# Window attention into two FF layers: group 4's softmax, five weight conversions and the second batch's v means written at other places

## The chip, the cores and the metric

The kernel runs on one core of one Trainium2 chip. The metric is device time in microseconds (us), the median of the runs. A profiled execution records what each engine does: TensorE (PE; its weight loads stand apart as PEld), VectorE (DVE), ScalarE (ACT), GpSimd (POOL) and SyncE (SP), which issues most DMAs.

## The reference, cut to what matters

```python
def _attn_ref(q, k, v):                       # (2, 8, 768, 64) each
    ...
    k_sum = k.reshape(B, H, nb, block, D).max(axis=3)      # block 32
    v_sum = v.reshape(B, H, nb, block, D).mean(axis=3)
    scores_l = scale * np.matmul(q, k.transpose(0, 1, 3, 2))
    mask_l = np.abs(pos[:, None] - pos[None, :]) < window  # 16
    scores_s = scale * np.einsum('bhsd,bhnd->bhsn', q, k_sum)
    scores_s = scores_s + np.log(block)
    scores_l_m = np.where(mask_l, scores_l, -1000000000.0)
    scores_all = np.concatenate([scores_l_m, scores_s], axis=-1)
    ...
    a = np.exp(scores_all)
    a = a / (np.sum(a, axis=-1, keepdims=True) + 1e-09)
    return np.matmul(a, np.concatenate([v, v_sum], axis=2))

def _moe_ref(x, w_in, w_out):                 # 1536 x 512, FF 2048
    h = np.maximum(x @ w_in, 0.0)
    return h * h @ w_out

def _moe2_ref(x, w_gate, w_val, w_out, rms_g):  # FF 1536
    ...
    return silu * val @ w_out
```

The result of the attention goes through `_moe_ref` and that through `_moe2_ref`.

## The kernel before

**Tiling.** The attention's 2 x 768 tokens are 12 groups of 128 tokens with all 8 heads; groups 0 to 5 are batch 0, groups 6 to 11 batch 1 (`GPB` is 6). A group has these steps: `scores` (32 matmuls into two PSUM tiles `s`), `softmax` (on VectorE two mask additions, a maximum `mx`; on ScalarE eight exponentials with sums, or for groups 5 and 9 a subtraction on VectorE and one exponential; then on VectorE the sum `sm` plus 1e-9, a reciprocal and the product `norm`), `ptrans` (8 transposes into two tiles `pps`, two ScalarE copies into `pT`), and `av` (32 matmuls into `xps`, then `xhi` by ScalarE and `xlo` by VectorE). `vload` loads a group's v rows into `vx`, which has four slots; groups alternate between slots 0, 1 and 2, 3, so a group's v rows cannot be loaded before the `av` of two groups earlier has read its slots. `qload` loads q for two groups, `qprep` transposes it (`qps`).

**FF layers.** Each fp32 operand is split into a high and a low part and each product is three matmuls (high by high, high by low, low by high). The first FF layer starts while the attention runs: its first round, four of 16 tiles of the inner size, goes over pairs of groups, `k_` from 0 to 5. For a pair `h_pair(k_, 0)` and `h_pair(k_, 2)` compute two inner tiles each (24 matmuls of 256 columns into `h0_k_f`; ScalarE takes the relu and VectorE the square, `r`; ScalarE `hhi` and VectorE `hlo` split it), and `y_pair(k_, 0)` and `y_pair(k_, 2)` multiply by the output weights (12 matmuls of 512 columns each). The attention of groups 4 to 11 is written between these calls. Behind the last pair, the rest of the first layer and the second run without attention.

**Weights.** A weight unit (`wi`, `wo`, later `wg`, `wv`, `wp`) is loaded raw as 64-bit words on SP's queue (512 KB), turned into fp32 by ScalarE (`conv_a`: `x`, `u`) and VectorE (`conv_b`, the "clamps": two tensor-scalars, L210 and L211, a scalar-tensor-tensor, L214, an integer addition, L217) and then split (`split`: a ScalarE cast, L223, and a VectorE subtraction, L224). Units 0 to 3 are `wi0` to `wi3`, units 4 to 7 `wo0` to `wo3`, and behind them come `wi4`, `wi5`, `wi6`, `wo4`, `wi7` and so on.

**What sets the order.** Every engine runs its instructions in one row. The row is made when the program is built: a scheduler takes the instructions as written and places each by an estimate of when it could start, so an instruction can move past others of its engine. `after(marks)` pins an instruction behind marked ones. The dictionary `FIRST` holds such pins for the units: the key (1, n) is `conv_a` of unit n, (2, n) is `conv_b`. PSUM tiles of the attention rotate through two tags with two buffers each, so the fifth tile reuses the buffer of the first.

The v means of batch 1 (`vs_mean`, `vmput`) are one matmul over `vsum`, which DMAs sum up, a VectorE copy and a GpSimd copy into `vx`.

Names such as `h0_3_0` read as pair 3, first tile; `xps1_8` is group 8's `av`. I call the time up to the start of group 5's transposes (71.57 us) stage 1, the time to the start of `h0_2_0` (82.87) stage 2, to the second part of `h0_3_0` behind group 10's q transposes (113.60) stage 3, and to the `xlo` matmul of `h0_4_0` (129.92) stage 4.

Of the kernel before, what the change touches and what calls it, by code (L numbers as in the profile page):

```python
# [15 lines left out]
ALU = mybir.AluOpType  # L16
# [16 lines left out]
def tile_window_attention_moe_moe2(  # L33
# [13 lines left out]
    nc = tc.nc  # L47
# [17 lines left out]
    GPB = S // P  # L65
# [154 lines left out]
    def split(x, nm):  # L220
# [4 lines left out]
        return hi, lo  # L225

    FIRST = {
        (2, 0): [("mx", 0)], (2, 2): [("mx", 2)], (2, 3): [("xlo", 1, 1)],
        (1, 1): [("qT", 2), ("pT", 1)], (1, 2): [("xhi", 0, 1)], (1, 3): [("exp", 2)],
    }  # L230

# [97 lines left out]
    mark = {}  # L329

    def after(*marks):
        es = ExitStack()
        for m in marks:
            es.enter_context(tc.issue_after(mark[m].ins))
        return es
# [74 lines left out]

    def vs_mean(b):
        ps = psA(f"vmean{b}", [K1, DM])[G0:K1]
        with after(("tr", GPB)):
            nc.tensor.matmul(ps, indv, vsum.rearrange("p h d -> p (h d)"), start=True, stop=True)
        vm = ap_.tile([K1, DM], F32, tag="vm", name=f"vm{b}", bufs=1)[G0:K1]
        state["vm"] = vm
        nc.vector.tensor_copy(vm, ps)
# [4 lines left out]
    def qload(g):  # L422
        b, r = divmod(g, GPB)
        state[("q", g)] = token_chunk(q, b, r // 2, f"qr{g}")
# [36 lines left out]
    def vmput(i0, n):  # L461
        nc.gpsimd.tensor_copy(vrows(i0, n), state["vm"].unsqueeze(1).to_broadcast([NB, n, DM]))
# [16 lines left out]
    def scores(g):  # L479
        b, r = divmod(g, GPB)  # L480
        qT = state[("qT", g)][:, :, (r % 2) * P : (r % 2 + 1) * P]
        sl = [psA(f"s{e}_{g}", [P, NPAIR, NK]) for e in range(2)]
        wide = [P, NPAIR, NK]
        if g < NPE:
            for s_ in sl:
                mh = mhi["mid" if r else "first"]
                nc.tensor.matmul(s_, identr, mh.unsqueeze(1).to_broadcast(wide), start=True, stop=False)
        for p in range(NPAIR):
            for x in range(2):
                for e in range(2):  # L490
                    u = (e + x) % 2
                    o = STEP * (2 * r + u)
                    rr = slice(QT * e, QT * e + QT)
                    with after(*((("av", 1),) if g == 3 else ())):
                        mark[("s", g)] = nc.tensor.matmul(  # L495
                            sl[e][QT * u : QT * u + QT, p, :],
                            qT[rr, p, QT * u : QT * u + QT],
                            kT[rr, p, o : o + NK],
                            start=g >= NPE, stop=g >= NPE,
                        )  # L500
        if g < NPE:
            for s_ in sl:
                mark[("s", g)] = nc.tensor.matmul(
                    s_, identr, mlo.unsqueeze(1).to_broadcast(wide), start=False, stop=True
                )
        state[("s", g)] = sl
# [44 lines left out]
    def ptrans(g):  # L551
        t = state.pop(("t", g))
        pT = ap_.tile([NK, H, P], F32, tag="pT", name=f"pT{g}", bufs=2)
        for hf in range(2):
            ps = psA(f"pps{g}_{hf}")
            for j in range(4):
                mark[("tr", g)] = nc.tensor.transpose(  # L557
                    ps[0:NK, j * P : (j + 1) * P], t[:, 4 * hf + j, :], ident
                )
            mark[("pT", g)] = nc.scalar.copy(pT[:, 4 * hf : 4 * hf + 4, :], ps[0:NK].rearrange("n (h s) -> n h s", h=4))  # L560
        state[("pT", g)] = pT
# [158 lines left out]
    def group(g):  # L720

        scores(g)
        if g > 3:
            vload(g)
        softmax(g)
        if g + 2 < NG and g % 2 == 0:
            qload(g + 2)
# [71 lines left out]
    def square(ps, nm):  # L799
        t = t2(f"r{nm}")  # L800
        nc.scalar.activation(t, ps, AF.Relu)  # L801
        nc.vector.tensor_tensor(t, ps, t, op=ALU.mult)  # L802
        return t


# [4 lines left out]
    def h_pair(k_, f):  # L810
        ps = psB.tile([P, CH], F32, tag="h", name=f"h0_{k_}_{f}", bufs=2)
        m = 2 * k_ % MT
        for j in range(2):
            units1.until(("wi", f + j))
            product(ps[:, G2 * j : G2 * (j + 1)], W[("wi", f + j)], xs[(1, 2 * k_ // MT)], m, m + 2)
        t = square(ps, f"0_{k_}_{f}")
        hq[(k_, f)] = hsplit(t, CH, f"0_{k_}_{f}")
# [22 lines left out]
    for k_ in range(NK2):  # L840
        g, last = 2 * k_ + 3, 2 * k_ + 3 >= NG
        h_pair(k_, 0)
        if k_ == 0:
            av(2)
            group(4)
        if not last:
            ptrans(g)
        h_pair(k_, 2)
        if not last:
            av(g)  # L850
        if g == GPB - 1:
            group(GPB)
        if g + 2 < NG:
            group(g + 2)
            if k_ == 0:
                for c in range(NC2):
                    prep_load(1, c)
                vs_load(1)
        y_pair(k_, 0)
        if g + 1 < NG:  # L860
            ptrans(g + 1)
        if g + 1 == GPB:
            vs_mean(1)
            vmput(0, 4)
        if k_ == 0:
            prep_begin(1)
            prep_k(1, 0)
            y_pair(k_, 2, (lambda: prep_k(1, 1), lambda: prep_k(1, 2)))
            prep_kend(1, nc.vector, 0, NW1)
        else:  # L870
            if g + 3 < NG:
                qprep(g + 3)
            y_pair(k_, 2)
        if g + 1 < NG:
            av(g + 1)
        if k_ == 0:
            qprep(GPB)
        elif g + 3 < NG:
            group(g + 3)
        if k_ == 2:  # L880
            units1.cap = NW - 3
            units1.load(units1.cap)
            units1.lim = len(units1.units)
            units1.behind = (("exp", 9), ("norm", 9))
        if k_ == NK2 - 1:
            units1.behind = ()
        for _ in range(TICKS[k_]):
            units1.tick()
        if not last and g == NG - 1:
            actx.close()  # L890
            rot["tags"] = ("a",)
            side["cb"] = ctx.enter_context(
                tc.tile_pool(name="cbpool", bufs=1, side="right", reuse_waits="tile")
            )
            grow = side["cb"].tile([P, DM], F32, tag="grow", name="grow")
            side["pool"] = hand.enter_context(
                tc.tile_pool(name="w2pool", bufs=1, side="right", reuse_waits="tile")
            )
            side["psum"] = ctx.enter_context(
                tc.tile_pool(name="psY2", bufs=1, space=PSUM, reuse_waits="tile")  # L900
            )
            nc.sync.dma_start(grow, rms_g.partition_broadcast(P))
            units1.cap = NW + NRIGHT - 3
# [256 lines left out]
```

## Time and profile before

| | us |
|---|---|
| median of 3 runs | 639.9 (639.51 to 640.55) |
| profiled execution | 640.56 |
| its span | 638.9 |
| PE busy | 623.5 (98%) |
| DVE busy | 458.3 (72%) |
| ACT busy | 365.0 (57%) |

The profiled execution is 1.66 longer than its span and 0.66 longer than the median. A matmul's row gives its own duration, which overlaps the next one's; the cost of a matmul in a sequence is the distance between starts. "Idle before" is the time that the engine stood, with the instruction that it waited for. PEclk is the granted clock of TensorE as a share of 2.4 GHz.

### The profile page before, as it was taken

What the parts mean: (1) busy time and instruction counts of PE and PEld (TensorE: products, weight loads), DVE (VectorE), ACT (ScalarE), POOL (GpSimd) and SP (SyncE); (2) the same over time, 40 slices, a digit from 0 to 9 for tenths busy, and PEclk for the clock granted to TensorE, in tenths of its full rate; (3) what the DMA queues carried; (4) which work ended last, traced back from release to release, by engine and by line L of the source; (5) the groups of instructions that cost most, each with busy time, mean ns of one, the idle gap of its engine ahead of it and who ended that gap; (6) DMA issues with size and microseconds to landing.
All of it is one profiled execution on the core that took longest, in us unless ns stands there. A gap on an engine that the chain in (4) does not pass through costs nothing.

```text
span 638.9 us, 9548 instructions
## 1 busy us (share of the span) xinstructions
PE 623.5 (98%) x3578; PEld 516.4 (81%) x3578; DVE 458.3 (72%) x831; ACT 365.0 (57%) x767; POOL 54.8 (9%) x81
## 2 busy tenths in 40 slices
PE   8988998999999999999999999999999999999997
PEld 6577887888888888888888888888888888888886
DVE  4799777959995289986486889489499399561323
ACT  5795566867673266564553767457367277353241
POOL 4012110000000000000000000003004004012040
PEclk9998998999999999999999999999999999999999
DMA  9999813615233123320020115218428329017063
GB/s 250 299 203 207 169 25 83 193 39 179 85 102 96 34 66 100 99 67 34 0 72 29 34 45 186 67 36 179 115 67 166 99 65 184 16 13 118 1 95 103
DMA packets 85870, 64.19 MB, mean 100 GB/s; under 512 B 51904, under 2 KB 75456, under 8 KB 85824
## 3 DMA queue, kind: packets, MB, share of 16 engines
q1 hardware_dynamic: 74576, 51.72, 27.5%
q0 software_dynamic: 11248, 11.87, 13.3%
q8 instruction: 28, 0.46, 0.3%
q14 instruction: 18, 0.15, 0.1%
HBM read 49.94 MB, written 13.63 MB: 100 GB/s over the span
## 4 chain that ended last, share of the span: by engine, by line
PE 88%; DVE 6%; DMA 2%; ACT 2%; SPq 1%; issue 1%
PE y L642 20%; PE h L620 19%; PE z L642 15%; PE qa L975 10%; PE v L620 5%; PE g L620 5%; PE qc L975 5%; PE qb L975 3%; DMA kr<-in_k_dram 1%; PE s L495 1%; PE pps L557 1%; PE xps L581 1%; PE xps L598 1%; DVE mx L531 1%; DMA vx<-in_v_dram 1%; DVE t L547 1%
## 5 line engine op out<-in xcount | busy, mean ns | idle before, releaser
L620 PE MATMUL h<-xhi,w_wi 128*128 128x512 f32 (+1 forms) x480 | 135.5, 355 | 4.5 <-ACT xhi L570 3.3
L642 PE MATMUL y<-w_wo,hhi 128*128 128x512 f32 x384 | 117.1, 393 | 1.1 <-ACT hhi L631 0.6
L620 PEld LDWEIGHTS h<-xhi,w_wi 128*128 128x128 f32 x480 | 87.0, 195 | 17.7 <-ACT xhi L570 4.4
L620 PE MATMUL h<-xlo,w_wi 128*128 128x512 f32 (+1 forms) x240 | 85.0, 355 | 1.6 <-DVE xlo L571 1.5
L642 PE MATMUL z<-w_wp,hhiz 128*128 128x512 f32 x288 | 85.8, 390 | 0.0
L642 PEld LDWEIGHTS y<-w_wo,hhi 128*128 128x128 f32 x384 | 71.4, 188 | 16.5 <-DVE w_wo L224 1.0
L1010 POOL DMA_DIRECT2D out_dram<-zs x40 | 35.5, 1173 | 493.1 <-ACT zs L1006 486.2
L642 PE MATMUL y<-w_wo,hlo 128*128 128x512 f32 x192 | 72.0, 391 | 0.0
L642 PEld LDWEIGHTS z<-w_wp,hhiz 128*128 128x128 f32 x288 | 53.9, 188 | 11.1
L620 PEld LDWEIGHTS h<-xlo,w_wi 128*128 128x128 f32 x240 | 46.8, 195 | 7.7 <-DVE xlo L571 2.2
L642 PE MATMUL z<-w_wp,hloz 128*128 128x512 f32 x144 | 53.0, 389 | 0.0
L801 ACT ACTIVATE r<-h 128x512 f32<-128x512 f32 x48 | 28.7, 599 | 40.1 <-PE h L620 40.1
L802 DVE TENSOR_TENSOR r<-h,r 128x512 f32<-128x512 f32 x48 | 32.8, 684 | 20.7 <-ACT r L801 20.7
L631 ACT CAST hhi<-r 128x512 fp32r<-128x512 f32 x48 | 29.9, 623 | 21.5 <-DVE r L802 21.2
L642 PEld LDWEIGHTS y<-w_wo,hlo 128*128 128x128 f32 x192 | 35.8, 188 | 7.4 <-issue 0.2
L632 DVE TENSOR_TENSOR hlo<-r,hhi 128x512 fp32r<-128x512 f32 x48 | 33.7, 702 | 10.0 <-ACT hhi L631 9.6
L620 PE MATMUL v<-x,w_wv 128*128 128x512 f32 x144 | 34.6, 389 | 0.0
L620 PE MATMUL g<-x,w_wg 128*128 128x512 f32 x144 | 34.6, 389 | 0.0
L1060 DVE TENSOR_TENSOR v<-qc,v 128x512 f32<-128x512 f32 x12 | 8.3, 691 | 36.4 <-ACT v L1059 36.4
L1006 ACT COPY zs<-z 128x512 f32<-128x512 f32 x48 | 26.8, 592 | 11.9 <-PE z L642 11.0
L642 PEld LDWEIGHTS z<-w_wp,hloz 128*128 128x128 f32 x144 | 27.0, 188 | 5.7
L620 PEld LDWEIGHTS g<-x,w_wg 128*128 128x128 f32 x144 | 27.0, 188 | 5.6
(205 smaller groups left out, 1216.1 us busy)
## 6 DMA issues: line engine op xcount, KB each, us to landing
out_dram<-zs POOLq DMA_DIRECT2D x40, 256.0 KB, 6.5
raw_wi<-in_moe_w_in_dram SPq DMA_DIRECT2D x16, 512.0 KB, 4.9
raw_wo<-in_moe_w_out_dram SPq DMA_DIRECT2D x16, 512.0 KB, 4.3
raw_wg<-in_moe_w_gate_dram SPq DMA_DIRECT2D x12, 512.0 KB, 3.6
raw_wv<-in_moe_w_val_dram SPq DMA_DIRECT2D x12, 512.0 KB, 3.5
raw_wp<-in_moe_w_out_dram SPq DMA_DIRECT2D x12, 512.0 KB, 5.4
kr<-in_k_dram SPq DMA_DIRECT2D x12, 256.0 KB, 4.2
qr<-in_q_dram SPq DMA_DIRECT2D x12, 256.0 KB, 4.9
```

Source lines behind the costliest of these rows:

```text
L495: mark[("s", g)] = nc.tensor.matmul(sl[e][QT * u : QT * u + QT, p, :], qT[rr, p, QT * u : QT * u + QT], kT[rr, p, o : o + NK], start=g >= ...
L531: mark[("mx", g)] = nc.vector.reduce_max(mx[:, NPAIR * e : NPAIR * (e + 1)], sl[e], axis=AX.X, negate=True)
L620: pe["last"] = nc.tensor.matmul(ps, a_, b_, start=(i == 0), stop=(i == tot - 1))
L631: nc.scalar.copy(hi[:, 0:n], s[:, 0:n]),
L632: nc.vector.tensor_tensor(lo[:, 0:n], s[:, 0:n], hi[:, 0:n].bitcast(F32), op=ALU.subtract),
L642: pe["last"] = nc.tensor.matmul(y, a_[:, ms], b_, start=(first and i == 0), stop=(last and i == 2))
L801: nc.scalar.activation(t, ps, AF.Relu)
L802: nc.vector.tensor_tensor(t, ps, t, op=ALU.mult)
L975: last = nc.tensor.matmul(ps, w[a_][:, kk], x[b_][:, kk], start=start and n == 0, stop=n == 3 * K2 - 1, skip_group_check=not start,)
L1006: nc.scalar.copy(s, ys.pop(m))
L1010: nc.gpsimd.dma_start(out[g * P : (g + 1) * P, :], s, accum_op=ALU.add)
L1060: nc.vector.tensor_tensor(v1[f], C[f], v1[f], op=ALU.add)
```

## The change

Three edits move work; nothing is added or taken away. `conv_b` of `wi2` (unit 2) waits for group 1's `xlo` instead of group 2's maximum, that of `wi3` and now of `wo0` (units 3 and 4) for group 2's `norm`, and those of `wo2` and `wo3` (units 6 and 7) for the square `r` of the pair `h0_0_2`. Group 4's softmax is written behind `h_pair(0, 2)` instead of ahead of it. The v means' matmul waits for group 7's scores instead of group 6's transposes, and its calls are written ahead of group 6's `ptrans`.

```diff
--- before.py
+++ after.py
@@ -225,7 +225,8 @@
         return hi, lo
 
     FIRST = {
-        (2, 0): [("mx", 0)], (2, 2): [("mx", 2)], (2, 3): [("xlo", 1, 1)],
+        (2, 0): [("mx", 0)], (2, 2): [("xlo", 1, 1)], (2, 3): [("norm", 2)], (2, 4): [("norm", 2)],
+        (2, 6): [("r", "0_0_2")], (2, 7): [("r", "0_0_2")],
         (1, 1): [("qT", 2), ("pT", 1)], (1, 2): [("xhi", 0, 1)], (1, 3): [("exp", 2)],
     }
 
@@ -410,7 +411,7 @@
 
     def vs_mean(b):
         ps = psA(f"vmean{b}", [K1, DM])[G0:K1]
-        with after(("tr", GPB)):
+        with after(("s", GPB + 1)):
             nc.tensor.matmul(ps, indv, vsum.rearrange("p h d -> p (h d)"), start=True, stop=True)
         vm = ap_.tile([K1, DM], F32, tag="vm", name=f"vm{b}", bufs=1)[G0:K1]
         state["vm"] = vm
@@ -799,7 +800,7 @@
     def square(ps, nm):
         t = t2(f"r{nm}")
         nc.scalar.activation(t, ps, AF.Relu)
-        nc.vector.tensor_tensor(t, ps, t, op=ALU.mult)
+        mark[("r", nm)] = nc.vector.tensor_tensor(t, ps, t, op=ALU.mult)
         return t
 
 
@@ -842,10 +843,14 @@
         h_pair(k_, 0)
         if k_ == 0:
             av(2)
-            group(4)
+            scores(4)
+            vload(4)
+            qload(6)
         if not last:
             ptrans(g)
         h_pair(k_, 2)
+        if k_ == 0:
+            softmax(4)
         if not last:
             av(g)
         if g == GPB - 1:
@@ -857,11 +862,11 @@
                     prep_load(1, c)
                 vs_load(1)
         y_pair(k_, 0)
-        if g + 1 < NG:
-            ptrans(g + 1)
         if g + 1 == GPB:
             vs_mean(1)
             vmput(0, 4)
+        if g + 1 < NG:
+            ptrans(g + 1)
         if k_ == 0:
             prep_begin(1)
             prep_k(1, 0)
```

The three places below are where the rows of an engine change. First VectorE around the square `r0_0_2`. In the names, `t4`, `mx4` and `sm4` belong to group 4's softmax, `x_wo2` and `x_wo3` to the conversions of the weights `wo2` and `wo3`. Before:

```order
L214 SCALAR_TENSOR_TENSOR x_wo2_814<-raw_wo2_355,x_wo2_814 128x512
L224 TENSOR_TENSOR w_wo1_824<-x_wo1_713,w_wo1_824 128x512
L214 SCALAR_TENSOR_TENSOR x_wo3_831<-raw_wo3_357,x_wo3_831 128x512
L217 ISA x_wo2_814<-x_wo2_814,u_wo2_815 128x1024
L217 ISA x_wo3_831<-x_wo3_831,u_wo3_832 128x1024
L545 TENSOR_SCALAR sm4_651<-sm4_651 128x8
L523 TENSOR_TENSOR t5_777<-s0_5_755,mask_last_187 128x480
L546 RECIPROCAL sm4_651<-sm4_651 128x8
L523 TENSOR_TENSOR t5_777<-s1_5_756,mask_last_187 128x480
L802 TENSOR_TENSOR r0_0_2_729<-h0_0_2_682,r0_0_2_729 128x512
L571 TENSOR_TENSOR xlo1_0_404<-xps1_3_736,xhi1_0_403 128x4x128
L547 TENSOR_TENSOR t4_649<-t4_649,sm4_651 128x960
```

After the change:

```order
L536 TENSOR_REDUCE mx4_720<-t4_719 128x8
L217 ISA x_wo1_696<-x_wo1_696,u_wo1_697 128x1024
L546 TENSOR_SCALAR sm4_721<-sm4_721 128x8
L547 RECIPROCAL sm4_721<-sm4_721 128x8
L548 TENSOR_TENSOR t4_719<-t4_719,sm4_721 128x960
L224 TENSOR_TENSOR w_wo1_824<-x_wo1_696,w_wo1_824 128x512
L524 TENSOR_TENSOR t5_777<-s0_5_755,mask_last_187 128x480
L803 TENSOR_TENSOR r0_0_2_712<-h0_0_2_665,r0_0_2_712 128x512
L210 TENSOR_SCALAR x_wo2_814<-x_wo2_814 128x512
L210 TENSOR_SCALAR x_wo3_831<-x_wo3_831 128x512
L524 TENSOR_TENSOR t5_777<-s1_5_756,mask_last_187 128x480
L572 TENSOR_TENSOR xlo1_0_404<-xps1_3_736,xhi1_0_403 128x4x128
```

Group 4's maximum, sum and `norm` (L548) now stand ahead of the subtraction of `w_wo1` and of the square, and the conversions of `wo2` and `wo3` stand behind the square. Group 4's softmax is not behind the square in the order that is built.

Second, TensorE at the end of stage 3, from group 6's `av` in the order before:

```order
L581 MATMUL xps1_6_1202<-pT6_1155,vx_93 64x64 x16
L495 MATMUL s1_8_1222<-kT_92,qT8_1173 64x120 x8
L581 MATMUL xps1_7_1340<-pT7_1295,vx_93 64x64
L495 MATMUL s1_9_1360<-kT_92,qT8_1173 64x120 x8
L557 MATMUL pps7_1_1302<-ident_78,t7_1124 120x128 x4
L495 MATMUL s0_9_1359<-kT_92,qT8_1173 64x120 x8
L581 MATMUL xps1_7_1340<-pT7_1295,vx_93 64x64 x15
L620 MATMUL h0_3_0_1515<-xhi1_1_947,w_wi0_555 128x256
L620 MATMUL h0_3_2_1560<-xhi1_1_947,w_wi2_683 128x256
L620 MATMUL h0_3_0_1515<-xlo1_1_948,w_wi0_555 128x256
```

After the change, from the last product of pair 2:

```order
L643 MATMUL y0_2_1_1394<-w_wo3_900,hlo0_2_2_1337 128x512
L496 MATMUL s0_9_1359<-kT_92,qT8_1173 64x120 x8
L582 MATMUL xps1_7_1340<-pT7_1295,vx_93 64x64 x15
L621 MATMUL h0_3_0_1515<-xhi1_1_947,w_wi0_555 128x256
L621 MATMUL h0_3_2_1560<-xhi1_1_947,w_wi2_666 128x256
L558 MATMUL pps8_0_1408<-ident_78,t8_1243 120x128 x4
L558 MATMUL pps8_1_1414<-ident_78,t8_1243 120x128 x4
L433 MATMUL qps10_0_1421<-ident_78,qr10_1260 128x128 x4
L433 MATMUL qps10_1_1427<-ident_78,qr10_1260 128x128 x4
L621 MATMUL h0_3_0_1515<-xlo1_1_948,w_wi0_555 128x256
```

Group 8's transposes (`pps8`) and group 10's q transposes (`qps10`) now stand directly behind the two first matmuls of `h0_3_0` and `h0_3_2`; before, the rest of `h0_3_0` stood between. Group 6's `av` and the first scores of groups 8 and 9 stand earlier, ahead of the second half of pair 2's products.

Third, SP's queue of DMA issues, behind group 9's v rows. Before:

```order
L192 DMA raw_wo4_1975<-in_moe_w_out_dram 128x1024
L188 DMA raw_wi7_1977<-in_moe_w_in_dram 128x4x256
L475 DMA vx_93<-in_v_dram 32x8x64
L475 DMA vx_93<-in_v_dram 64x8x64
L475 DMA vx_93<-in_v_dram 32x8x64
L475 DMA vx_93<-in_v_dram 64x8x64
L192 DMA raw_wo5_1979<-in_moe_w_out_dram 128x1024
```

After the change:

```order
L476 DMA vx_93<-in_v_dram 32x8x64
L476 DMA vx_93<-in_v_dram 64x8x64
L192 DMA raw_wo4_1975<-in_moe_w_out_dram 128x1024
L188 DMA raw_wi7_1977<-in_moe_w_in_dram 128x4x256
L192 DMA raw_wo5_1979<-in_moe_w_out_dram 128x1024
```

Group 10's four v loads moved ahead of the loads of `raw_wo4` and `raw_wi7`; those four wait for group 8's `av`, whose slots of `vx` they fill.

## Rows read from the trace of the kernel before

**Rows 1.** the page: busy us (share of the span) xinstructions

```profile
PE 623.5 (98%) x3578; PEld 516.4 (81%) x3578; DVE 458.3 (72%) x831; ACT 365.0 (57%) x767; POOL 54.8 (9%) x81
```

**Rows 2.** timeline of TensorE: start us, us, engine, line, op, operands, count [idle before]

```profile
51.83 0.50 PE L642 MATMUL y<-w_wo,hhi 128*128 128x512 f32 x1 [0.53 <-DVE w_wo L224]
...
71.57 0.60 PE L557 MATMUL pps<-ident,t 128*120 128x128 f32 x4
...
111.94 1.04 PE L557 MATMUL pps<-ident,t 128*120 128x128 f32 x8
...
113.60 0.36 PE L620 MATMUL h<-xlo,w_wi 128*128 128x256 f32 x1
...
125.91 1.21 PE L642 MATMUL y<-w_wo,hhi 128*128 128x512 f32 x4 [0.56 <-ACT hhi L631]
...
128.20 0.62 PE L642 MATMUL y<-w_wo,hhi 128*128 128x512 f32 x2
128.66 0.39 PE L642 MATMUL y<-w_wo,hlo 128*128 128x512 f32 x1
...
129.92 0.36 PE L620 MATMUL h<-xlo,w_wi 128*128 128x256 f32 x1
```

**Rows 3.** windows: us, length, busy PE PEld DVE ACT POOL, PEclk, DMA share, GB/s

```profile
53.20:55.60 2.40, 0.47 (x3) 0.22 (x2) 2.40 (x7) 2.34 (x7) 0.17 (x1) 1.00 1.30 233
56.40:59.80 3.40, 3.40 (x18) 3.40 (x17) 3.40 (x5) 0.00 (x0) 0.35 (x1) 0.50 1.10 150
104.60:107.60 3.00, 0.56 (x4) 0.32 (x3) 2.93 (x6) 2.98 (x12) 0.00 (x0) 1.00 0.43 98
107.60:111.10 3.50, 3.50 (x16) 3.50 (x17) 3.40 (x5) 3.00 (x6) 0.00 (x0) 0.51 0.54 178
29.10:32.50 3.40, 2.25 (x44) 1.52 (x41) 3.40 (x7) 2.81 (x13) 0.00 (x0) 1.00 1.03 413
```

**Rows 4.** timeline of VectorE, 45 to 75 us

```profile
48.16 0.41 DVE L211 TENSOR_SCALAR x_wo<-x_wo 128x512 uint32<-128x512 uint32 x1
...
49.10 1.14 DVE L535 TENSOR_REDUCE mx<-t 128x8 f32<-128x960 f32 x1
...
52.30 1.28 DVE L217 CUSTOM_DVE_ANT_0 x_wo<-x_wo,u_wo 128x1024 uint16<-128x1024 uint16 x2
53.51 0.15 DVE L545 TENSOR_SCALAR sm<-sm 128x8 f32<-128x8 f32 x1
...
67.68 1.88 DVE L384 TENSOR_REDUCE ksum<-kps 128x16 f32<-128x512 f32 x3
```

**Rows 5.** timeline of ScalarE, 45 to 75 us

```profile
50.30 0.38 ACT L537 ACTIVATE t<-t,mx 128x120 f32<-128x120 f32 x1
```

**Rows 6.** window from group 4's sm to the end of group 5's norm

```profile
53.51:67.68 14.17, 12.32 (x77) 11.39 (x78) 12.40 (x22) 6.55 (x15) 3.01 (x3) 0.88 1.14 218
```

**Rows 7.** tile vsum: its DMAs and the v means' matmul

```profile
L409 POOL DMA_DIRECT2D vsum<-in_v_dram x7: 1315/1315/1631, 36.1 to 74.9; - x7
...
L414 PE MATMUL vmean<-vsum,indv x2: 592/600/609, 88.8 to 89.2; 96*24 96x512 f32 x2
...
DMA to landing us min/median/max: 4.2/6.1/9.6
```

**Rows 8.** timeline of VectorE, 97 to 130 us

```profile
101.78 1.15 DVE L535 TENSOR_REDUCE mx<-t 128x8 f32<-128x960 f32 x1
...
107.44 1.15 DVE L547 TENSOR_TENSOR t<-t,sm 128x960 f32<-128x960 f32 x1
```

**Rows 9.** timeline of SyncE's queue, DMA issues, 70 to 130 us

```profile
106.51 0.61 SPq L192 DMA_DIRECT2D raw_wo<-in_moe_w_out_dram  x1
...
116.84 2.82 SPq L475 DMA_DIRECT2D vx<-in_v_dram  x4
```

**Rows 10.** tile raw_wo, 60 to 140 us, issue to landing

```profile
DMA to landing us min/median/max: 3.5/4.6/6.2
```

**Rows 11.** timeline of ScalarE, 97 to 130 us

```profile
118.14 0.69 ACT L203 ACTIVATE x_wo<-raw_wo 128x512 f32<-128x512 f32 x1
```

## The prediction

> **What bounds the kernel now.** First the page: PE is busy for 623.5 of 638.9 us [rows 1], so about 15.4 us are all that a new order can give back, and any order that makes PE stand longer costs at once. The change moves only work between 45 and 130 us, so I went through PE's timeline there for the places where it stands. In stage 1 there are three: 0.53 ahead of the products by `w_wo1` [rows 2], and, in the window from 53.2 to 55.6, 1.93 more (2.40 less 0.47 busy) [rows 3]. In stage 3 it is 2.44 of the 3.00 us from 104.6 [rows 3], and in stage 4 0.56 [rows 2]: 5.46 in all. Behind each of the two larger stands, the granted clock falls to the lower level, 1.2 GHz: 0.50 from 56.4 for 3.4 us and 0.51 from 107.6 for 3.5 us [rows 3]. Half of that time, about 1.65 each, is lost work. Where PE stood only 1.15 of 3.40 us (29.1 to 32.5, 2.25 busy), the clock stayed full [rows 3]. So some 8.8 us of the stretch can be gained or lost again. Then I read what VectorE and ScalarE do in these stretches, since they are what PE waits for, and walked the new rows of each engine by the starts of the old ones.
>
> **The change, stage 1.** In the order that is built, group 4's maximum no longer stands behind two L210s, one L211 and one L217 of other weights. A tensor-scalar of this shape costs 0.34 from start to start and an L217 0.60 [rows 4], so 1.6; some of it comes back as VectorE waits for its input, and I take 1.5. `mx4` goes from 49.10 [rows 4] to 47.6, and the eight exponentials from 50.30 [rows 5] to 48.8. They were done just ahead of `sm4` at 53.51 [rows 4], so they take 3.15, to 52.0. The bill: on ScalarE `w_wo1`'s cast, ahead of them before, now stands behind them. It ends at 52.5, while PE wants it at about 51.0: a stand of 1.5 in place of 0.53. VectorE has `sm4` next in its row behind one L217, so it stands from 49.4 to 52.0, and gets to `sm4` 1.5 earlier than at 53.51 [rows 4].
>
> From there VectorE carries more to the end of the stage. Before, from `sm4` (53.51) to the end of group 5's `norm` (67.68, where the next one starts) [rows 4] VectorE worked for 12.40 of 14.17 us [rows 6]. Now `w_wo1`'s subtraction is in that stretch (0.60), as are the conversions of `wo2` and `wo3` (twice 0.34 + 0.34 + 0.60 + 0.60, so 3.75), the three `ksum` reductions that stood behind `norm` (1.8) [rows 4], and two more of about 0.65: 7.45 in all. So `norm` ends at 52.0 + 12.4 + 7.5 = 71.9, not at 67.68. Group 5's transposes, which it releases and which came at 71.57 [rows 2] with PE as the limit, come at 72.05: **+0.5**. PE's own work would be done at about 70.1; it stands for some 1.95 there. The stands earlier in the stage, about 3.2 in all, are covered by this, and so is a fallen clock there: VectorE is the limit up to this point. By `h0_2_0` I count +0.7, for changes between kinds of matmul that now come more often: an estimate.
>
> **Stage 2** has no wait to lose: from 72 to 104 us PE's timeline shows none. The v means' matmul goes from 88.8 [rows 7] to about 84.5. The last DMA into their sum was issued at 74.9 [rows 7]; issued up to 1.3 later and landing in 4.2 to 9.6 [rows 7], it is there between 80.4 and 85.8. So the price is nothing to 1.3; I take nothing, as the median landing, 6.1, gives 82.3. GpSimd's copy moves with it, and nobody waits for that before group 6's `av`.
>
> **Stage 3.** Group 8's second scores stand ahead of 12 products of pair 2. At 0.23 each (128.20 to 128.66 for two) [rows 2] that is 2.75 earlier, less the 0.7 carried. So `mx8` starts at 99.7 in place of 101.78 [rows 8], the exponentials end at 103.95, and the first matmul of `h0_3_0` starts some 0.6 earlier than before. Yet group 8's transposes stand directly behind the first two matmuls now, and they need `norm8`. Before, that started at 107.44 [rows 8], with the same mask, maximum and subtraction of group 9 ahead of it on VectorE and with `xlo` too. Without `xlo` it is 0.55 earlier, with group 9's scores 0.3 later: it ends at 108.25. PE stands 0.4 (for `pT7`), 0.7 (for `xhi`) and 1.75 (for `norm8`): 2.85 of some 4.2 us. That is more standing than in either stretch that was followed by the lower clock (1.93, 2.44) and more than twice the 1.15 that was not, so I take a fall and its 1.65. From 108.3: transposes of both kinds 1.66 (111.94 to 113.60) [rows 2], 23 matmuls of 0.12, small switches, and 1.6 for the clock: 114.55. The same work was done at 113.60 [rows 2]: **+0.95**, or -0.65 with the clock up.
>
> The Trainium skill (TensorE: Matmul & The Clock Gate, Part 1: The HAM clock gate) says that the clock knows only two levels, and that the block which sets them watches in a rhythm of its own that doesn't begin with the kernel. The two levels are what [rows 3] shows; by the rhythm the fall of stage 3 would be a chance and not a certainty, and the time without it is the third case below.
>
> **Stage 4** is where SP's queue comes in. `raw_wo4` was issued at 106.51, 10 us ahead of group 10's v rows at 116.84 [rows 9], and ScalarE used it without a wait at 118.14 [rows 11]. Now it stands behind those four v loads, which wait for group 8's `av`. That ends at 115.0 by the walk; the four issues take 2.1 to 2.8, and a landing takes 3.5 to 6.2, median 4.6 [rows 10]. `raw_wo4` is there between 120.6 and 124, I take 121.2; ScalarE asks for it at about 118.0. Behind it in ScalarE's row stand `u_wo4`, a `pT` copy, `hhi0_3_0`, `u_wi7` (together with itself 2.8) and then group 10's exponentials (3.1), which end at 127.0. VectorE does `sm10`, `mx11`, the square and `xlo9` behind them (2.5), so `h0_4_0` goes on at 129.6. PE's own work ends at about 127.3: it stands 2.25, in place of 0.56 [rows 2]. Twelve products (2.75) and group 10's transposes (0.8) that had been done by 129.92 [rows 2] are still to come: 133.1, **+3.2** in all. Behind that, order and work are those of before, and PE has no waits.
>
> The sum is 640.56 + 3.2 for an execution such as the profiled one; on the median, 0.66 lower, 639.9 + 3.2 = **643.1**. Bounds: a landing between 120.6 and 124 makes 642.5 to 645.9.
>
> **The rivals.** (1) *The clock falls once more.* The stand of 1.95 ahead of group 5's transposes is as long as the 1.93 that was followed by half speed, and the 2.25 ahead of `h0_4_0` is longer. Against it: each is one stand with full work on both sides. Each costs 1.65: 644.7, both 646.4. (2) *One of the two prices of stages 3 and 4 isn't paid.* If the clock stays up, group 8's `av` ends 1.65 earlier and the v loads with it: 641.5. If `raw_wo4` comes in time after all, PE's own row is the limit: 127.3 + 3.55 = 130.85, +0.9: 640.8. (3) *Faster: VectorE isn't the limit in stage 3.* Its place is `norm8`. If it ends by 106.6, since group 9's scores come 1.7 earlier than I walked, PE doesn't stand, the clock stays up, group 8's `av` and the loads come early enough that ScalarE isn't held, and 0.65 + 0.56 are won: 638.7. With the other stands of stage 3 gone as well, 1.8 more: 636.9. For it speaks that `mx8` and its exponentials are 2 us earlier; against it, that `norm8` has the same four long instructions ahead of it. (4) *The change doesn't do what its words say.* On group 4 that is so already: its softmax isn't behind the square in the built row. It has its price in the sum above, and no other.
>
> **How the numbers follow.** Forecast 0.38 (its own range 642.5 to 645); rival 1 0.20; rival 2 0.20, half of it at 641.5 and half at 640.8; rival 3 0.17; 0.05 elsewhere. The range from 638.2 to 645.8 leaves out most of rival 3 and the top of rival 1, about 0.18. A measurement of this kernel can tell about 0.2% from no change, 1.3 us: below 638.6 lies most of rival 3, 0.15; up to 641.2 lie half of rival 2 and the rest, 0.14; above 0.71.
>
> **What would show it.** After: PE waits about 1.5 for `w_wo1`'s cast near 51; VectorE stands some 2.6 ahead of `sm4` and then not at all to group 5's `norm`, which ends near 72; the transposes of group 8 wait for `norm8` near 108, and the granted clock is about 0.5 behind that; SP issues `raw_wo4` near 117.5 and ScalarE stands for it some 3 us. If that last wait isn't there, or PE is full from 104 to 108, the forecast is wrong. It would also be wrong if stretches behind 133 us differ.

## The result, and the profile after

The median of six runs was 646.69 us (644.26 to 650.03), beside 640.13 (639.51 to 641.03) for six runs of the kernel before on the same chip: a ratio of 1.0103 [1.0075, 1.0132], slower by some 6.6 us. The forecast was 643.1, slower by 3.2; the time lies above its range. The profiled execution took 647.04, its span 645.3: 6.48 longer than the one of before. Below, a time "of before" belongs to the rows that stand ahead of the prediction.

The page first: busy us (share of the span) xinstructions, to be held against [rows 1].

```profile
PE 624.5 (97%) x3578; PEld 516.2 (80%) x3578; DVE 460.0 (71%) x831; ACT 365.4 (57%) x767; POOL 54.8 (8%) x81
```

PE is busy 1.0 longer, and stands 20.8 us (645.3 less 624.5) in place of 15.4. So 5.4 of the 6.4 us of span are standing.

Where it stands, the timeline of TensorE from 40 to 140 us shows (start us, us, engine, line, op, operands, count, [idle before <- what ended it]); these are the rows that answer to [rows 2].

```profile
40.92 1.04 PE L496 MATMUL s<-kT,qT 64*64 64x120 f32 x16 [0.55 <-ACT qT L435]
...
53.16 0.73 PE L643 MATMUL y<-w_wo,hhi 128*128 128x512 f32 x2 [1.44 <-ACT w_wo L223]
...
72.90 1.06 PE L558 MATMUL pps<-ident,t 128*120 128x128 f32 x8 [1.80 <-DVE t L548]
...
84.17 0.28 PE L621 MATMUL h<-xhi,w_wi 128*128 128x256 f32 x1
...
105.19 1.15 PE L582 MATMUL xps<-pT,vx 120*64 120x64 f32 x30 [0.31 <-ACT pT L561]
107.02 0.51 PE L621 MATMUL h<-xhi,w_wi 128*128 128x256 f32 x2 [0.67 <-ACT xhi L571]
109.19 1.94 PE L558 MATMUL pps<-ident,t 128*120 128x128 f32 x8 [1.66 <-DVE t L548]
...
125.74 1.15 PE L582 MATMUL xps<-pT,vx 120*64 120x64 f32 x30 [1.80 <-ACT pT L561]
...
131.12 0.38 PE L621 MATMUL h<-xhi,w_wi 128*128 128x256 f32 x1 [0.94 <-ACT xhi L571]
132.19 0.36 PE L621 MATMUL h<-xhi,w_wi 128*128 128x256 f32 x1 [0.68 <-DVE r L803]
132.70 0.39 PE L621 MATMUL h<-xlo,w_wi 128*128 128x256 f32 x1 [0.15 <-DVE xlo L572]
```

Read it by stages. Group 5's transposes start at 72.90, 1.33 later than before, behind a stand of 1.80. Pair 2's first tile starts at 84.17, 1.30 later than the 82.87 of before: stage 2 adds nothing. In stage 3, PE stands 0.31, 0.67 and 1.66, the last for group 8's `norm`, which stands behind group 9's maximum and subtraction in VectorE's row:

```profile
105.62 1.15 DVE L542 TENSOR_REDUCE mx<-t 128x8 f32<-128x960 f32 x1
...
107.89 1.15 DVE L548 TENSOR_TENSOR t<-t,sm 128x960 f32<-128x960 f32 x1
```

In stage 4 there are four stands, 3.57 in all, where before had one of 0.56. `h0_4_0` goes on at 132.70. The work that before had done by 129.92 [rows 2] takes 3.55 more (the twelve products and group 10's transposes of the prediction), so the delay there is 132.70 + 3.55 - 129.92 = 6.3: all of it. SP's next raw loads come at 153.04 where before had them at 146.56, the same 6.5.

The granted clock, by windows (us, length, busy PE PEld DVE ACT POOL, PEclk, DMA share, GB/s), beside [rows 3]:

```profile
107.90:114.40 6.50, 5.21 (x25) 5.25 (x26) 6.40 (x14) 5.76 (x10) 0.00 (x0) 0.50 0.20 46
...
73.00:80.00 7.00, 7.00 (x111) 5.40 (x111) 4.95 (x8) 3.55 (x7) 0.00 (x0) 1.00 1.20 279
```

From 107.9, inside the stand of 1.66, it is 0.50, the 1.2 GHz level, for 6.5 us with 5.21 of work in them: half of that, 2.6, is lost. Behind the stand of 1.80 at 72.9 it stays at 2.4 GHz in this execution.

Last, SP's queue and ScalarE in stage 4, beside [rows 9] and [rows 11]. SyncE:

```profile
78.58 40.68 SPq L476 DMA_DIRECT2D vx<-in_v_dram  x16
119.31 0.62 SPq L192 DMA_DIRECT2D raw_wo<-in_moe_w_out_dram  x1
...
153.04 3.09 SPq L192 DMA_DIRECT2D raw_wo<-in_moe_w_out_dram  x3
```

ScalarE, 112 to 134 us:

```profile
119.64 0.58 ACT L561 COPY pT<-pps 120x512 f32<-120x512 f32 x1
124.00 0.66 ACT L203 ACTIVATE x_wo<-raw_wo 128x512 f32<-128x512 f32 x1 [3.77 <-DMA raw_wo<-in_moe_w_out_dram]
124.56 0.66 ACT L204 ACTIVATE u_wo<-raw_wo 128x512 int32<-128x512 uint32 x1
125.11 0.57 ACT L561 COPY pT<-pps 120x512 f32<-120x512 f32 x1
...
127.00 0.38 ACT L538 ACTIVATE t<-t,mx 128x120 f32<-128x120 f32 x1
...
130.51 0.57 ACT L571 CAST xhi<-xps 128x512 fp32r<-128x512 f32 x1
```

`raw_wo4` is issued behind the v loads at 119.31 and used 4.69 later. ScalarE stands 3.77 for it, with the second `pT` copy of group 9 behind it in its row; PE's 1.80 at 125.74 is the wait for that copy. Group 10's exponentials follow from 127.00 to 130.13, and behind them the `xhi` cast that PE's 0.94 at 131.12 waits for.

### The profile page after: what moved, and what is told of

It reads as the page before. It is cut to its first block, busy times and chain, and to the rows that moved or that the text cites. A ratio compares the mean times of both kernels' runs of the same rounds, so it can differ in the third digit from the quotient of the medians.

```text
span 645.3 us, 9544 instructions
## 1 busy us (share of the span) xinstructions
PE 624.5 (97%) x3578; PEld 516.2 (80%) x3578; DVE 460.0 (71%) x831; ACT 365.4 (57%) x767; POOL 54.8 (8%) x81
## 4 chain that ended last, share of the span: by engine, by line
PE 87%; DVE 6%; SPq 3%; DMA 2%; ACT 2%; issue 1%; DVEq 0%; ACTq 0%
PE y L643 19%; PE h L621 18%; PE z L643 15%; PE qa L980 10%; PE v L621 5%; PE g L621 5%; PE qc L980 5%; PE qb L980 3%; SPq L359 2%; PE s L496 2%; PE pps L558 1%; PE xps L582 1%; DMA raw_wi<-in_moe_w_in_dram 1%; ACT t L538 1%; PE xps L599 1%; DMA qr<-in_q_dram 1%
## 5 line engine op out<-in xcount | busy, mean ns | idle before, releaser
L621 PEld LDWEIGHTS h<-xhi,w_wi 128*128 128x128 f32 x480 | 85.5, 191 | 16.2 <-ACT xhi L571 2.5
```

Source lines behind the costliest of these rows:

```text
L621: pe["last"] = nc.tensor.matmul(ps, a_, b_, start=(i == 0), stop=(i == tot - 1))
```

## The experiments

My theory after the result: two prices make the loss, the wait of ScalarE for `raw_wo4` and the wait for group 8's `norm` with the low clock behind it. The first rival: VectorE's conversions of `wo2` and `wo3` in stage 1 bring group 5's transposes late, and through that (or a fallen clock behind that stand) all the rest. The first four kernels undo one thing in the changed kernel; the next do one thing alone in the kernel before. Ratios are to the kernel before on the same chip; 0.1% is 0.64 us.

**`late_x`: the changed kernel with unit 11 (`wo4`) and 12 converted on ScalarE only behind group 10's exponentials.**

```diff
+        (1, 11): [("exp", 10)], (1, 12): [("exp", 10)],
```

> The changed kernel, but the first ScalarE step of wo4 and wi7 (x, u) is pinned behind group 10's exponentials; the loads stay where they are on SP's queue, late. Theory (ScalarE stands 3.8 us for raw_wo4 with pT9 and the exponentials of group 10 queued behind it, and PE pays 1.80 + 1.77 for that): both stands of PE go, 646.7 - 3.4 = 643.3 (642.3 to 644.3). Rival (the wait is covered, the loss is the low clock and VectorE in stages 1 and 3): no change, 646.2 to 647.2.

Measured: 642.35 (10 runs, 641.26 to 647.84), 1.0049 [1.0026, 1.0073]. ScalarE no longer waits, though the load is issued at 121.84, later still, and PE has no stand in stage 4:

```profile
128.79 0.65 ACT L203 ACTIVATE x_wo<-raw_wo 128x512 f32<-128x512 f32 x1
```

So this wait is worth 0.54% or 3.5 us, about the 3.57 of PE's stands there. The stands of 1.67 for `norm8` and of 1.49 for group 5's `norm` remain. The execution profiled was a long one, 645.68. It has a low clock behind the latter, from 75.3 to 82.0 with PE full, and two more low stretches (0.50 from 42 to 51, 0.61 from 112.6 to 117). TensorE's row at 73.32 is `pps`, eight transposes:

```profile
73.32 1.06 PE L559 MATMUL pps<-ident,t 128*120 128x128 f32 x8 [1.49 <-DVE t L549]
...
73.40:81.00 7.60, 7.60 (x56) 5.36 (x58) 3.75 (x7) 2.71 (x5) 1.31 (x1) 0.63 1.13 245
75.30:82.00 6.70, 6.70 (x52) 4.79 (x52) 3.57 (x5) 1.21 (x3) 0.13 (x1) 0.50 1.12 259
```

**`norm8_first`: the changed kernel with group 9's maximum behind group 8's `norm` on VectorE.**

```diff
-                nc.vector.reduce_max(m_, tv, axis=AX.X)
+                with after(*((("norm", 8),) if g == 9 else ())):
+                    nc.vector.reduce_max(m_, tv, axis=AX.X)
```

> The changed kernel with group 9's maximum pinned behind group 8's norm; norm 8 then loses the 2.05 us of group 9's maximum and subtraction ahead of it. In the order that results, x of wo4 stands behind group 10's exponentials too. Theory: the stand for raw_wo4 goes (3.4), PE's stand of 1.66 for norm 8 shrinks to nothing or a little, and if the clock then stays up some 2.6 more: 641.6 with the low clock, 639.0 without it. Rival (norm 8 isn't what holds PE there, or group 9's transposes come late in its place): 643 or more.

Measured: 641.50 (10 runs, 640.38 to 646.71), 1.0030 [1.0007, 1.0053]. The stand for `norm8` halves and the clock stays at 2.4 GHz behind it. TensorE's row, the window, and ScalarE's two steps on `raw_wo4`:

```profile
107.32 1.06 PE L559 MATMUL pps<-ident,t 128*120 128x128 f32 x8 [0.91 <-DVE t L549]
...
107.30:113.00 5.70, 5.68 (x77) 5.30 (x81) 4.07 (x6) 4.64 (x8) 0.00 (x0) 1.00 0.26 59
...
127.53 0.68 ACT L204 ACTIVATE u_wo<-raw_wo 128x512 int32<-128x512 uint32 x1 [2.04 <-DMA raw_wo<-in_moe_w_out_dram]
128.12 0.66 ACT L203 ACTIVATE x_wo<-raw_wo 128x512 f32<-128x512 f32 x1
```

That is 4.7 us better than the change. But in the order that this builds, ScalarE's work on `raw_wo4` has moved too: it stands behind group 10's exponentials, `x_wo4` at 128.12, and the 2.04 that ScalarE still waits for the load hold up no `pT` copy of group 9 and no exponential of group 10. Of the 4.7, 3.5 may be that; the 1.2 that is left for `norm8` and the clock is not shown by itself, since the intervals of the two kernels overlap.

**`no_clamp67`: the changed kernel without the pins of `wo2` and `wo3`.**

```diff
-        (2, 6): [("r", "0_0_2")], (2, 7): [("r", "0_0_2")],
```

> The changed kernel without the pins of wo2 and wo3 behind the square. In the order that results, their conversions stand ahead of the square again, and x of wo4 stands behind group 10's exponentials. Theory: the stand for raw_wo4 goes (3.4) and VectorE's long chain to group 5's norm too (0.9): about 642.4 (641.2 to 643.5). Rival 1 (all of the loss comes from the two conversions that stand behind the square): 640.1. Rival 2 (the late load costs nothing): 645.4 or more.

Measured: 640.43 (10 runs, 639.62 to 642.81), 1.0004 [0.9990, 1.0017]: the rival's number. This one line carries 0.99%. PE has no stand in front of group 5's transposes and is busy for 39.40 of the 40.00 us from 94 to 134. ScalarE still waits for the load, and PE then 1.45 for the copy behind it. TensorE's one stand in stage 1, ScalarE's wait, and the two windows from 94 us:

```profile
54.03 1.13 PE L642 MATMUL y<-w_wo,hhi 128*128 128x512 f32 x2 [2.26 <-ACT w_wo L223]
...
127.98 0.66 ACT L203 ACTIVATE x_wo<-raw_wo 128x512 f32<-128x512 f32 x1 [3.46 <-DMA raw_wo<-in_moe_w_out_dram]
...
94.00:114.00 20.00, 20.00 (x256) 16.70 (x253) 14.28 (x22) 13.64 (x35) 0.00 (x0) 1.00 0.24 54
114.00:134.00 20.00, 19.40 (x176) 17.22 (x175) 18.76 (x35) 13.91 (x47) 0.00 (x0) 1.00 0.55 173
```

This kernel too has more than one thing undone. Its `x_wo4` stands behind group 10's exponentials, and on VectorE group 8's `norm` stands ahead of group 9's maximum, the order that `norm8_first` pins; in the change it stands behind:

```profile
104.52 1.15 DVE L547 TENSOR_TENSOR t<-t,sm 128x960 f32<-128x960 f32 x1
...
106.18 1.14 DVE L541 TENSOR_REDUCE mx<-t 128x8 f32<-128x960 f32 x1
```

**`no_first`: the changed kernel with the old pins of units 2 and 3 and none for unit 4.**

```diff
-        (2, 0): [("mx", 0)], (2, 2): [("xlo", 1, 1)], (2, 3): [("norm", 2)], (2, 4): [("norm", 2)],
+        (2, 0): [("mx", 0)], (2, 2): [("mx", 2)], (2, 3): [("xlo", 1, 1)],
```

> The changed kernel with the old pins for wi2, wi3 and wo0. In the order that results wo2's and wo3's conversions stay behind the square, and x of wo4 stands behind group 10's exponentials. Theory: the stand for raw_wo4 goes, the rest stays: 643.3 (642 to 645). Rival (these pins have no part in it): 646.7.

Measured: 641.59 (10 runs, 639.68 to 645.70), 1.0037 [1.0011, 1.0063], 1.7 below what was expected. Six runs lie at 639.7 to 642.3 and four at 644.0 to 645.7. Here too `norm8` (103.83) stands ahead of group 9's maximum (106.16), and `x_wo4` (127.39) behind group 10's exponentials. The profiled one, 640.07, has a stand of 1.94 ahead of group 5's transposes and full clock behind it:

```profile
72.38 1.06 PE L558 MATMUL pps<-ident,t 128*120 128x128 f32 x8 [1.94 <-DVE t L548]
...
72.40:80.00 7.60, 7.60 (x98) 6.14 (x99) 5.04 (x8) 3.28 (x6) 1.19 (x1) 1.00 1.02 236
```

**`no_vmean`: the changed kernel with the v means at their old place and pin** (the last two edits of the diff reversed).

```diff
-        with after(("s", GPB + 1)):
+        with after(("tr", GPB)):
```

> The changed kernel without the v means' edit. In the order that results stage 1 and the place of raw_wo4 on SP's queue are those of the changed kernel; x and u of wo4 and u of wi7 stand ahead of group 10's exponentials and of group 9's pT copies. Theory: the stand for raw_wo4 stays, with more queued behind it: 646.5 to 648.5. Rival (the v means' matmul is what pushes stage 3): 645 or less.

Measured: 653.93 (4 runs, 652.58 to 656.70), 1.0209 [1.0176, 1.0242]: slower by 6.8 us than the change, and far outside what was expected. ScalarE waits 4.55 for the load and PE 4.68 for the copy behind it. So the new place of the v means gains in this company. That is not the load's wait alone: the granted clock is 0.51 from 108 to 115 and 0.55 from 130 to 136.

Next, the parts alone, in the kernel before.

**`only_clamp67`.**

```diff
+        (2, 6): [("r", "0_0_2")], (2, 7): [("r", "0_0_2")],
...
+        mark[("r", nm)] = nc.vector.tensor_tensor(t, ps, t, op=ALU.mult)
```

> The kernel before with one edit alone: wo2's and wo3's conversions pinned behind the square. In the order that results VectorE's row around the square, SP's queue (raw_wo4 behind group 10's v rows) and ScalarE's (x of wo4 ahead of group 10's exponentials) are like those of the changed kernel. Theory (this edit carries the loss, by the late load and VectorE's chain): 645 to 647.5. Rival (the loss needs the other edits too): below 643.

Measured: 649.58 (4 runs, 648.55 to 650.10), 1.0134 [1.0110, 1.0157], and by another way than expected. `x_wo4` waits for nothing here. PE stands 1.94 ahead of group 5's transposes, as in `no_first`, but now the clock is at 1.2 GHz for the 14 us behind it:

```profile
72.93 1.72 PE L558 MATMUL pps<-ident,t 128*120 128x128 f32 x8 [1.94 <-DVE t L548]
...
73.00:80.00 7.00, 7.00 (x42) 5.26 (x42) 3.02 (x5) 2.70 (x5) 0.84 (x1) 0.51 0.87 204
80.00:87.00 7.00, 7.00 (x62) 5.79 (x59) 2.88 (x4) 2.40 (x10) 0.48 (x1) 0.51 0.59 88
```

14.0 times 0.49 is 6.9 us lost, more than the 1.65 at which the prediction priced a fall.

**`only_first`: the new pins of units 2, 3 and 4 alone, and `only_first_late`, the same with the line of `late_x`.**

```diff
-        (2, 0): [("mx", 0)], (2, 2): [("mx", 2)], (2, 3): [("xlo", 1, 1)],
+        (2, 0): [("mx", 0)], (2, 2): [("xlo", 1, 1)], (2, 3): [("norm", 2)], (2, 4): [("norm", 2)],
```

> The kernel before with the new pins of wi2, wi3 and wo0 alone. In the order that results raw_wo4 stands behind group 10's v rows, and x of wo4 ahead of group 10's exponentials; wo2's and wo3's conversions stay ahead of the square. Theory: the stand for raw_wo4, +3.4: 643.5 (642 to 645). Rival (these pins, which were loosened or moved by a few instructions only, change nothing): 639.5 to 641.2.

Measured: 648.63 (4 runs), 1.0134 [1.0107, 1.0160]; the size was short by 5 us. The wait for the load is longer than in the change. So is PE's for the copy, which stands behind group 10's exponentials in this order:

```profile
125.42 0.66 ACT L203 ACTIVATE x_wo<-raw_wo 128x512 f32<-128x512 f32 x1 [4.18 <-DMA raw_wo<-in_moe_w_out_dram]
...
130.18 1.97 PE L581 MATMUL xps<-pT,vx 120*64 120x64 f32 x30 [5.14 <-ACT pT L560]
```

> The kernel before with the new pins of wi2, wi3 and wo0, and with x and u of wo4 and wi7 pinned behind group 10's exponentials. Without that second pin ScalarE stood 4.18 us for raw_wo4 and PE 5.14 for pT9 behind it. Theory (that stand is the larger part of this kernel's +8.6): 648.6 - 5.1 = 643.5 (642.3 to 645). Rival (the stand is paid elsewhere anyway): 647 or more.

Measured: 644.90 (4 runs), 1.0064 [1.0046, 1.0081]. With `x_wo4` behind the exponentials (127.93, no wait) 0.7%, 4.5 us, come back: the second pair of kernels that shows the price of this wait. The clock was low in both profiles (0.74 from 130.2 to 137 in the first, 0.59 from 109 to 117 in the second), so the 4.5 are not the stand alone.

**`only_vmean`: the v means' edit alone, and `only_vmean_late`, the same with the line of `late_x`.**

```diff
-        with after(("tr", GPB)):
+        with after(("s", GPB + 1)):
...
-        if g + 1 < NG:
-            ptrans(g + 1)
         if g + 1 == GPB:
             vs_mean(1)
             vmput(0, 4)
+        if g + 1 < NG:
+            ptrans(g + 1)
```

> The kernel before with the v means' edit alone. In the order that results raw_wo4 stands behind group 10's v rows and u and x of wo4 ahead of group 10's exponentials, while VectorE's row around the square is that of before. Theory: the stand for raw_wo4 alone, +3.4: 643.5 (642 to 645). Rival (the late load matters only where the stages ahead were late already): 640 to 641.3.

> The kernel before with the v means' edit, and with x and u of wo4 and wi7 pinned behind group 10's exponentials. Without that second pin ScalarE stood 4.25 us for raw_wo4, yet PE only 1.07 + 0.43 in stage 4; its granted clock was 0.72 from 104 to 112 and 0.64 from 112 to 120, 5.1 us of lost work in place of 1.7. Theory (here stage 3's stands and the low clock behind them carry the loss): 646.8 - 1.5 = 645.3 (644.3 to 646.5). Rival (the late load carries the same 3.4 as in the changed kernel): 643.4.

Measured: 646.81 (4 runs), 1.0091 [1.0065, 1.0118], and 643.88 (5 runs), 1.0050 [1.0032, 1.0067]. Alone, the edit that I had put at nothing costs 5.8 us; some 2.6 of them go with ScalarE's wait for the load. The second lies below the theory's range and 0.5 above the rival's number; its interval does not shut out the theory's 645.3.

**`only_soft4`: group 4's softmax at its new place, alone.**

```diff
-            group(4)
+            scores(4)
+            vload(4)
+            qload(6)
...
+        if k_ == 0:
+            softmax(4)
```

> The kernel before with group 4's softmax alone written behind the pair's second tile. In the order that results its sum and norm stand behind the square, and raw_wo4 ahead of group 10's v rows as in before. Theory: no late load, so nothing to lose in stage 4; group 4's norm some 1 us later in stage 1, mostly covered: 640.2 (639.5 to 641.5). Rival (a later norm 4 is what delays the pair's products): 642 or more.

Measured: 642.75 (10 runs), 1.0035 [1.0020, 1.0051], not the no change that was expected; the number is the rival's. The profile shows another way to it: a `pT` copy of group 9 stands behind group 10's exponentials, PE waits for it, and the clock behind that is 0.66 from 125 to 130.

```profile
125.01 1.15 PE L581 MATMUL xps<-pT,vx 120*64 120x64 f32 x30 [1.68 <-ACT pT L560]
```

Yet inside the whole change this edit does nothing: without it the same row is built on every engine.

**`before_norm8` and `late_load`: a late load in the kernel before.** The first has the edit of `norm8_first`; the second pins the load behind group 8's `av`.

```diff
+                with after(*((("av", 8),) if u == ("wo", 4) else ())):
+                    self.raw[u] = load64(*u)
```

> The kernel before with group 9's maximum pinned behind group 8's norm. There PE stands for group 7's xhi, which ScalarE does behind group 8's exponentials, and not for norm 8; x of wo4 stands behind group 10's exponentials in this order, so that the late load is covered. Theory: no change, 640.1 (639 to 641.3). Rival (norm 8 bounds stage 3 in that kernel too): 637.5 to 638.8.

> The kernel before, with the order of every engine as it was, but the load of raw_wo4 waits for group 8's av, as it does in the changed kernel; raw_wi7 and group 10's v rows stay behind it. Theory (the late load is a cost by itself, since group 10's exponentials and pT9 stand behind x of wo4 on ScalarE): ScalarE stands some 3.7 us at x of wo4, and the time is 640.1 + 3.3 = 643.4 (642.3 to 644.5). Rival (it costs only together with the other delays): 640 to 641.2.

Measured: 641.23 (10 runs), 1.0019 [1.0002, 1.0035], and 640.44 (12 runs), 0.9999 [0.9984, 1.0015]. In the first the load is issued at 115.98, 9.5 later than before, and `x_wo4` runs without a wait at 125.61 behind the exponentials: a late load by itself costs little where ScalarE asks late. The second pin ordered nothing: every engine's row is that of the kernel before, and `raw_wo4` went out at 106.40, as before (106.51): `after` places an instruction within the row of its own engine, and the load is SyncE's, the `av` TensorE's. So it says nothing of the load; it is a second measurement of the kernel before, good to 0.15%.

**`best_try`: the changed kernel without the pins of `wo2` and `wo3`, and with `wo4`'s conversion on ScalarE behind group 11's exponentials.**

```diff
-        (2, 6): [("r", "0_0_2")], (2, 7): [("r", "0_0_2")],
+        (1, 11): [("exp", 11)], (1, 12): [("exp", 11)],
```

> The changed kernel without the pins of wo2 and wo3, and with x and u of wo4 and wi7 pinned behind group 11's exponentials. Without that second pin (no_clamp67) ScalarE stood 3.46 us for raw_wo4 ahead of group 11's exponentials and PE 1.45 for group 10's pT behind them. Theory: the 1.45 goes and nothing takes its place: 640.3 - 1.45 = 638.9 (638.2 to 639.8), a ratio of 0.998. Rival (PE waits as long for another product of VectorE, or w_wo4 comes late for the second round): 640 or more.

Measured: 639.68 (12 runs, 638.29 to 640.51), 0.9978 [0.9966, 0.9989] of the kernel before: faster by about 1.4 us. From 96 to 136 us PE is full at 2.4 GHz, through all of stages 3 and 4, and `x_wo4` waits for nothing:

```profile
96.00:136.00 40.00, 40.00 (x433) 34.67 (x434) 33.12 (x56) 28.41 (x83) 0.00 (x0) 1.00 0.36 106
...
132.27 0.65 ACT L203 ACTIVATE x_wo<-raw_wo 128x512 f32<-128x512 f32 x1
```

What is left in stage 1 is a stand of 2.94 for `w_wo1`'s cast and 0.30 behind it, at 55 us, where the kernel before stood 2.46 (0.53, 1.16 and 0.77).

## Why the prediction was wrong

The direction and the places were right, the size was half: 3.2 in place of 6.6, because three terms of the sum were too small. The low clock of stage 3 cost 2.6 and not 1.65, `raw_wo4` took 4.69 from issue to use and not 3.7, and stage 1 ended later than its +0.5. The steps of the sum, with the delay against before at the end of each:

| | forecast | measured |
|---|---|---|
| stage 1, to group 5's transposes | +0.5 | +1.33 |
| to `h0_2_0` (stage 2) | +0.7 | +1.30 |
| group 8's transposes start | 108.3 | 109.19 |
| stage 3, the work of 113.60 | +0.95 | +3.0 |
| issue of `raw_wo4`; its use | 117.5; 121.2 | 119.31; 124.00 |
| `h0_4_0` goes on | 129.6 | 132.70 |
| stage 4, the work of 129.92 | +3.2 | +6.3 |

The forecast of the issue is the prediction's "near 117.5". For stage 3, the matmul of `h0_3_0` that stood at 113.60 has its place in the new row at 118.95, and ahead of it stand now 2.32 us that came later before (group 8's `av`, 0.26 and 1.08, and scores, 0.98): 116.63.

**Stage 1: the limit was right, its start late.** PE stands 1.44 for `w_wo1` (forecast 1.5), and VectorE 2.60 ahead of `sm4` (forecast some 2.6). VectorE's timeline:

```profile
52.63 0.17 DVE L546 TENSOR_SCALAR sm<-sm 128x8 f32<-128x8 f32 x1 [2.60 <-ACT t L538]
...
71.62 1.14 DVE L548 TENSOR_TENSOR t<-t,sm 128x960 f32<-128x960 f32 x1
```

From `sm4` to the end of group 5's `norm` it took 72.76 - 52.63 = 20.1; the sum had 19.9. Only `sm4` came at 52.63 and not at 52.0. Of that 0.63, 0.36 was there already at group 4's scores (40.92 in place of 40.56), ahead of where I began to walk. It is not shown to come from the new pins of units 2 and 3: `no_clamp67` and `only_first` have them and start those scores at 40.49 and 40.53. The 0.2 that the sum gave stage 2 for changes between kinds of matmul doesn't show (+1.33 becomes +1.30). This is 0.6 of the 3.1 that the forecast was short by.

**Stage 3: the low clock was mis-sized.** PE stood 1.66 for `norm8` (forecast 1.75), and the clock fell, as forecast. But I gave the fall the length of the two that before shows, some 3.5 [rows 3], and 1.65 (half of them is 1.7); it lasted 6.5 and cost 2.6. That is 0.95 of the shortage; another 0.5 lies in where `norm8` ended (109.04; the sum had 108.25, and its own terms make 108.34) and in the row behind it. The profile of before has two low stretches, of 3.4 and 3.5, and that of the change this one of 6.5: the low time is about the same in all, but now the whole of it lies in stage 3.

**Stage 4: the wait was forecast, the load too early.** The stand of 3.77 on ScalarE was forecast as some 3. `h0_4_0` goes on 3.1 later than the sum had it, in three parts. `raw_wo4` was issued at 119.31 and not near 117.5: 1.8, handed on by stage 3. It was used 4.69 later, about the median of [rows 10], 4.6, where the sum took 3.7 (117.5 to 121.2), less than that median: 1.0. From its use to `h0_4_0` it took 8.7, and the sum had 8.4: 0.3. So stage 4 added 3.3, not 2.25: 1.05 of the shortage, most of it the landing. The use at 124.00 is the prediction's late bound to the hundredth, but by luck: that bound stood for a slow landing, and a late issue made it.

The sum went along ScalarE's row to group 10's exponentials and did not price the `pT` copy that stands closer behind the load, for which PE stands 1.80. By the rows this moves a stand more than it adds one: the `xhi` cast of group 9 comes behind the exponentials either way, and what PE does not stand for the copy it would stand at 131.12. No run has the copy alone moved. `late_x` and `only_first_late` show that the wait is a cause, and 3.5 and 4.5 us large; in the pairs of `only_vmean` and of `best_try` it is 2.6 and 1.7. It is the largest term, as the prediction had it.

**Rival 1 was priced too low.** Behind the same stand ahead of group 5's transposes the clock held in the profiles of the change (1.80), `no_first` (1.94) and `norm8_first` (1.80). It fell in `late_x` (1.49; at 0.50 from 75.3 to 82.0, beginning 2.0 us behind the stand) and in `only_clamp67` (1.94; 0.51 for 14). So the fall is a chance, and the work lost by it here was 3.4 (half of 6.7) to 6.9, not 1.65. By the Trainium skill (TensorE: Matmul & The Clock Gate, Part 1: The HAM clock gate) the block that sets the clock watches in a rhythm of its own; that 1.94 held in one kernel and fell in another agrees with it.

Every run's mean granted clock was measured too. In `no_first` the four long runs have 0.981 to 0.986 and the six others 0.992 to 1.000, so in one and the same program a low clock goes with some 5 us (medians 645.4 and 640.3); where in those runs it fell is not known. In `late_x` it is less clear: 0.983, 0.984 and 0.991 for the three long runs (645.7 to 647.8), 0.986 to 1.000 for the others (641.3 to 643.0). The spread of the change itself does not go with the clock: its longest run, 650.03, has 0.989, its shortest, 644.26, has 0.992, and the lowest, 0.988, belongs to 645.77.

**Rivals 2 to 4.** Neither price was spared, and VectorE was the limit of stage 3. Group 4's softmax indeed never stood behind the square, and the edit has no share in the change's time.

**Which edit.** Without the pins of `wo2` and `wo3` 6.3 us are gone. That is not shown to be the price of VectorE's extra work in stage 1. `no_clamp67`, `no_first` and `norm8_first` share two orders that the change has not: `norm8` ahead of group 9's maximum, and `x_wo4` behind group 10's exponentials. The last two of them keep the pins of `wo2` and `wo3` and stand 1.94 and 1.80 ahead of group 5's transposes, and yet are 4.2 and 4.7 us better than the change; their profiled executions took 640.07 and 640.76. So most of the 6.3 goes with the orders of stages 3 and 4, which are built otherwise as soon as these pins go, or those of units 2 to 4 (`no_first`). The 1.7 between `norm8_first` and `no_clamp67` are not clear of the noise. This answers the first rival of the experiments: a late start of group 5's transposes with the clock up does not by itself bring the rest; with a fallen clock behind it, it is dear (`only_clamp67`).

What stays open is how the 3.1 us that remain in `late_x` divide between stage 1's delay, `norm8` and the low clock: no run has `norm8` alone moved with `x_wo4` where the change has it. Open too is why the parts alone cost 0.35% to 1.34% each, 3.9% in sum, where all together cost 1.03%. That each builds another order is seen; which of its differences makes the price was followed only at the waits shown above.

## What to carry to other kernels

When a load moves back in its queue, look at its first user and then at everything behind that user in its engine's row, up to the last thing that TensorE needs from there; putting the user further back can win most of the price back. Take the landing at the median that the rows show. Price a fall of the clock as a chance with a length between the shortest and the longest seen, and not at the length of one row. Edits that pass through a scheduler do not add up: taking one away can turn other orders round as well, so compare the rows that are built with and without it before giving it a price.

## What the runs showed of the hardware

A stand of TensorE of 1.5 to 1.9 us was followed by no fall of the clock (`no_first`, 1.94), by 6.7 us at 0.50 (`late_x`, 1.49) or by 14 us at 0.51 (`only_clamp67`, 1.94), with TensorE fully busy all the while in the last two. A full row of work did not bring the clock back for 14 us, where before it was back after some 3.5 [rows 3]. One program, `no_first`, ran at a mean granted clock of 0.992 to 1.000 six times and of 0.981 to 0.986 four times, and some 5 us longer then.
